# New issue order and bank assignment for a linformer attention + gated FFN kernel on Trainium2

## The chip, the cores and the metric

The kernel runs on one core of one Trainium2 chip. The metric is the device time of one execution in microseconds (us), the median of several runs. Engines are named as in the profile: PE is TensorE's matmuls and PEld its weight loads, DVE is VectorE, ACT is ScalarE, POOL is GpSimd, SP is SyncE.

## The reference

Attention with projected keys and values, and then a gated feed-forward layer on the heads joined together. Cut to what matters:

```python
# q, k, v: (8, 8, 1024, 64); E, F: (64, 1024)
k_proj = np.einsum('ks,bhsd->bhkd', E, k)
v_proj = np.einsum('ks,bhsd->bhkd', F, v)
scores = q @ k_proj.transpose(0, 1, 3, 2) / np.sqrt(64)
attn = np.exp(scores - scores.max(-1, keepdims=True))
attn = attn / (attn.sum(-1, keepdims=True) + 1e-9)
x = (attn @ v_proj).transpose(0, 2, 1, 3).reshape(8192, 512)
# w_gate, w_val: (512, 1536); w_out: (1536, 512)
gate = 1.0 / (1.0 + np.exp(-(x @ w_gate)))
out = (gate * (x @ w_val)) @ w_out          # (8192, 512), float32
```

## The kernel before

The eight batches are worked on in a software pipeline. While the feed-forward layer of one batch runs, the attention of the next is computed and the inputs of the one after that are loaded. Matmuls are in bfloat16 and add up in the eight PSUM banks `pF0..3` and `pA0..3` (128 x 512 float32 each).

Attention, per batch: GpSimd issues six loads with conversion to bfloat16 (jobs `loadkv` four times, for K and V in halves of four heads, into `KVs`; `loadq` twice, into `Qb`; L560). SyncE transposes Q by DMA (`turnq`, `qT<-Qb`). TensorE projects K and V (`kv`, `KVs,EFT`) once all four K/V halves have landed; then come the scores (`sc`), VectorE's maximum and its subtraction (`top`, `sub`), ScalarE's exponential (`exp`, into `KVs`, which then serves as `pt`), a DMA transpose (`turnp`, `eT<-KVs`), the products with V (`xo`), the division by the sum (`div`: on VectorE from PSUM, or on GpSimd from a copy in SBUF) and a second DMA transpose (`turnx`, `xT<-KVs`), which gives the layer's input `xT`. The loads of a later batch go into the same `KVs`, so they wait for the `turnx` transposes.

The feed-forward layer, per block of 512 tokens: the products with `w_gate` and `w_val` are done for six row tiles at a time with seven products of half-size blocks in place of eight (function `seven`; job names such as `GA11`, `VS3`, `GS4`). This takes sums of blocks of the input (`xs`, `xS<-xT`, four per block of tokens: one on GpSimd and three on VectorE for most blocks), additions of partial results (`plus` on VectorE, `snap` and `copy` on ScalarE), the tanh form of the sigmoid (`tanh` on ScalarE, into buffers `spare` and `EF` in SBUF) and the product gate times value (`hidden`, VectorE, L1216, `hT<-spare,...`). `hidden` reads the value from PSUM in three of the four quarters, and in the fourth (half 1, token half 1) from an SBUF buffer: then both of its inputs lie in SBUF. The output product with `w_out` is done the same way (`OA11`, `OS2` and so on), with the sums `sum1`, `sum2`, `sum3` on VectorE and `sum4` on GpSimd (L548, `hT<-hT,hS`), `merge` on VectorE and `leave` on ScalarE, and SyncE's stores of 256 KB. For the first and the last of the sixteen blocks the output product is a plain one (`Oplain`).

The order of the work is a table. The program first registers 2,902 jobs, each with its engine and its body, and then `Scheduler.run` gives every PSUM bank and SBUF buffer that a job needs its place from `PLACES` (906 entries: banks 0 to 7, buffers 0 to 12) and returns the jobs' bodies in the order of `ORDER` (2,937 entries: each job once, and 35 times -1, which stands for a filling matmul that keeps TensorE at work in the first microseconds):

```python
        for s, p in zip(slots, PLACES):
            s.at = p
        return [fill if i < 0 else self.jobs[i].body for i in ORDER]
```

`Plan.add` then derives from the order which instruction must wait for which, and each engine runs its own instructions in that order. So the table fixes five queues at once, and where a job stands among the jobs of other engines tells the time at which the table's author expects it to start.

Jobs that the prediction names, by number: loads 399, 650, 1018, 1022, 1386, 2123 (GpSimd, L560); additions 1036 and 1772 (`xs` on GpSimd, L548); `sum3` 1271, `hidden` 1565 and `sum2` 2006 (VectorE).

Of the kernel before, what the change touches and what calls it, by code (L numbers as in the profile page):

```python
# [153 lines left out]
class Job:  # L154
# [5 lines left out]
    0, -1, -1, -1, 1, 2, 3, -1, -1, -1, -1, -1, -1, 12, 4, 13, 14, 5, -1, -1, 6, 15, 16, 22, 17, -1, -1, 7, 23,  # L160
    18, 8, 19, -1, -1, -1, 24, 34, 9, 20, 25, -1, -1, 10, 32, 35, 11, 26, 33, 27, -1, -1, -1, -1, -1, -1, -1,
    -1, -1, 36, 42, 52, 37, 21, -1, -1, -1, 38, 53, 39, 43, 30, 54, 40, 28, 31, 44, 59, 55, 29, 45, 168, 41, -1,
    56, 46, 48, 57, 60, 47, 58, 169, 49, 61, -1, -1, -1, -1, 50, 62, 112, 346, 51, 119, 63, 165, 113, 64, 65,
    164, 118, 120, 174, 124, 122, 121, 126, 175, 129, 123, 128, 177, 125, 130, 178, 131, 114, 68, 116, 66, 176,
    115, 69, 67, 86, 117, 70, 87, 88, 71, 180, 76, 89, 136, 127, 96, 77, 179, 90, 144, 72, 78, 145, 181, 73, 91,
    79, 148, 146, 167, 80, 138, 133, 74, 150, 152, 92, 75, 97, 149, 93, 154, 147, 81, 140, 98, 153, 94, 166,
    142, 99, 137, 151, 95, 155, 132, 100, 82, 134, 84, 182, 101, 102, 85, 161, 103, 83, 160, 190, 184, 106, 186,
    162, 183, 104, 139, 108, 141, 107, 188, 135, 301, 105, 143, 185, 109, 302, 163, 198, 303, 111, 278, 110,
    187, 214, 199, 172, 262, 170, 304, 200, 192, 215, 171, 204, 201, 173, 216, 189, 305, 202, 217, 263, 218,
    196, 203, 220, 191, 264, 279, 395, 205, 219, 266, 265, 193, 221, 396, 206, 280, 222, 230, 207, 267, 209,  # L170
    225, 281, 210, 211, 223, 231, 269, 197, 208, 246, 212, 227, 270, 232, 226, 247, 234, 228, 233, 236, 213,
    224, 248, 235, 250, 397, 273, 251, 237, 229, 253, 308, 238, 249, 294, 254, 239, 309, 252, 398, 295, 243,
    240, 241, 255, 296, 307, 257, 244, 297, 282, 242, 256, 259, 306, 283, 537, 258, 298, 285, 260, 245, 538,
    286, 531, 299, 274, 261, 156, 300, 533, 289, 535, 158, 157, 194, 290, 323, 310, 159, 314, 319, 337, 311,
    332, 426, 315, 312, 316, 313, 320, 317, 429, 324, 318, 333, 325, 334, 326, 328, 427, 338, 423, 430, 321,
    335, 339, 322, 329, 340, 327, 539, 195, 268, 330, 424, 341, 271, 347, 331, 351, 425, 284, 431, 348, 342,
    354, 349, 275, 336, 352, 432, 355, 287, 356, 272, 357, 343, 428, 288, 350, 344, 353, 345, 276, 291, 433,
    359, 532, 366, 363, 358, 367, 360, 549, 534, 368, 361, 292, 369, 550, 277, 434, 364, 365, 362, 371, 546,
    293, 375, 378, 372, 547, 370, 373, 379, 536, 380, 540, 376, 548, 377, 381, 383, 390, 551, 374, 391, 384,
    392, 552, 385, 386, 541, 382, 553, 387, 545, 555, 393, 388, 389, 556, 543, 394, 415, 499, 557, 435, 500,  # L180
    515, 416, 436, 521, 554, 418, 501, 516, 417, 437, 439, 438, 544, 519, 517, 520, 503, 502, 505, 399, 504,
    522, 518, 440, 457, 542, 506, 523, 442, 507, 524, 526, 401, 421, 558, 419, 400, 510, 508, 528, 420, 511,
    402, 512, 529, 443, 441, 422, 509, 513, 451, 446, 527, 452, 559, 403, 444, 447, 455, 514, 525, 404, 467,
    445, 448, 530, 456, 453, 449, 483, 454, 458, 484, 473, 560, 459, 489, 487, 563, 468, 460, 561, 462, 450,
    461, 469, 488, 471, 766, 485, 463, 472, 464, 470, 474, 490, 486, 475, 669, 491, 476, 685, 670, 478, 465,
    477, 480, 492, 494, 479, 671, 493, 409, 672, 481, 686, 495, 406, 482, 466, 687, 770, 410, 496, 768, 564,
    673, 688, 405, 411, 675, 765, 674, 689, 413, 497, 691, 412, 676, 690, 498, 771, 677, 769, 407, 692, 414,
    678, 733, 693, 749, 767, 408, 734, 680, 694, 679, 682, 735, 681, 695, 696, 750, 683, 772, 736, 697, 751,
    773, 565, 737, 566, 774, 738, 752, 583, 684, 775, 567, 569, 584, 779, 776, 740, 698, 568, 570, 753, 741,
    585, 574, 578, 571, 744, 586, 780, 754, 579, 587, 572, 575, 781, 745, 573, 580, 596, 782, 756, 576, 592,  # L190
    581, 785, 562, 588, 577, 701, 757, 593, 582, 786, 702, 597, 760, 787, 589, 705, 703, 598, 590, 789, 704,
    594, 591, 739, 599, 761, 601, 790, 595, 602, 699, 603, 608, 600, 605, 706, 707, 609, 604, 606, 607, 717,
    791, 708, 700, 610, 778, 718, 617, 613, 742, 755, 709, 721, 614, 618, 611, 758, 615, 719, 722, 619, 712,
    616, 743, 612, 620, 720, 724, 625, 621, 746, 759, 622, 783, 713, 623, 747, 725, 629, 784, 626, 710, 777,
    627, 624, 728, 630, 788, 711, 714, 628, 748, 631, 637, 795, 762, 638, 796, 729, 792, 639, 715, 640, 644,
    632, 641, 793, 633, 763, 634, 716, 905, 635, 642, 645, 764, 646, 906, 647, 643, 636, 723, 794, 867, 667,
    803, 648, 868, 726, 883, 804, 869, 665, 907, 900, 730, 798, 666, 805, 870, 797, 727, 668, 871, 806, 731,
    807, 872, 819, 732, 808, 809, 899, 874, 810, 902, 875, 908, 901, 650, 811, 878, 903, 649, 873, 879, 812,
    914, 876, 651, 820, 814, 813, 816, 652, 815, 880, 817, 823, 654, 884, 881, 821, 818, 835, 653, 822, 824,
    885, 882, 887, 886, 826, 836, 904, 851, 877, 799, 837, 801, 827, 839, 888, 889, 838, 830, 909, 852, 831,  # L200
    890, 840, 911, 855, 891, 915, 913, 892, 857, 856, 800, 894, 893, 802, 858, 842, 895, 853, 843, 917, 859,
    910, 846, 916, 896, 847, 862, 912, 897, 841, 863, 918, 844, 1037, 659, 860, 845, 854, 898, 657, 861, 825,
    660, 848, 1134, 658, 864, 828, 661, 919, 849, 1038, 662, 920, 663, 829, 1039, 865, 921, 1041, 655, 850,
    1133, 832, 1040, 1053, 922, 1042, 923, 656, 833, 1054, 926, 1136, 1135, 1055, 1044, 866, 1057, 1056, 927,
    1058, 834, 924, 1137, 1043, 925, 928, 1060, 1045, 1101, 931, 1061, 1059, 1046, 930, 664, 1117, 932, 1062,
    933, 1047, 929, 1048, 934, 1064, 1049, 1138, 1050, 1102, 935, 1066, 1139, 1063, 936, 1103, 1051, 1118, 1140,
    1065, 1052, 937, 1067, 1104, 1105, 1119, 1141, 938, 1121, 1120, 946, 1122, 1142, 939, 1106, 942, 1124, 947,
    940, 1143, 943, 1125, 941, 1108, 948, 1147, 1146, 951, 1148, 1109, 944, 949, 955, 952, 1144, 1112, 945,
    1149, 953, 1113, 950, 960, 956, 1150, 964, 1069, 954, 957, 1153, 1070, 965, 1154, 958, 961, 1071, 1155, 959,
    969, 1073, 962, 1072, 1157, 970, 966, 963, 973, 1128, 971, 1068, 967, 1158, 972, 1129, 1074, 968, 976, 981,  # L210
    1085, 1159, 982, 974, 977, 1123, 975, 1086, 1076, 1126, 983, 985, 1087, 978, 986, 984, 987, 988, 1089, 989,
    993, 1088, 990, 1130, 979, 1077, 1107, 994, 1131, 995, 1145, 1000, 1080, 980, 1001, 1110, 997, 1002, 1091,
    1090, 998, 991, 1075, 999, 1092, 1078, 996, 1009, 992, 1114, 1093, 1010, 1082, 1011, 1111, 1003, 1151, 1115,
    1079, 1096, 1081, 1127, 1004, 1152, 1116, 1097, 1012, 1005, 1156, 1273, 1006, 1274, 1094, 1164, 1007, 1083,
    1160, 1008, 1275, 1013, 1098, 1132, 1014, 1235, 1015, 1033, 1171, 1236, 1161, 1016, 1172, 1034, 1237, 1084,
    1162, 1173, 1238, 1035, 1239, 1166, 1095, 1174, 1187, 1165, 1240, 1175, 1099, 1251, 1188, 1268, 1242, 1176,
    1267, 1191, 1243, 1269, 1178, 1192, 1246, 1270, 1179, 1189, 1271, 1022, 1247, 1194, 1190, 1182, 1018, 1195,
    1241, 1272, 1252, 1167, 1282, 1036, 1244, 1253, 1100, 1255, 1017, 1254, 1198, 1256, 1193, 1168, 1183, 1019,
    1177, 1258, 1180, 1020, 1248, 1259, 1196, 1276, 1245, 1021, 1249, 1184, 1257, 1025, 1199, 1262, 1185, 1203,
    1219, 1163, 1260, 1204, 1026, 1283, 1263, 1181, 1277, 1250, 1205, 1220, 1279, 1200, 1281, 1221, 1186, 1201,  # L220
# [1685 lines left out]
```

## Time and profile before

| what | value |
|---|---|
| median of three runs | 524.64 us (524.38 to 524.77) |
| the profiled execution's own time | 523.46 us |
| its span, first to last instruction | 521.7 us |
| TensorE busy in the span | 510.9 us |
| VectorE, ScalarE, GpSimd busy | 446.4, 374.5, 171.3 us |
| granted TensorE clock | 1.00 |
| DMA | 71.57 MB; 148 GB/s of HBM over the span |
| last matmul to the span's end | about 2.7 us (ScalarE's copy and the last store) |

Other lines that matter, GpSimd's groups by shape (line, engine, operation, output<-inputs, shapes, count; busy us, mean ns; idle time before them and what ended it):

```profile
L548 POOL TENSOR_TENSOR hT<-hT,hS 128x512 bf16<-128x512 bf16 x42 | 50.2, 1211 | 188.7 <-PE pF L519 87.5 <-PE pA L519 85.3 <-DVE xS L548 15.9
L548 POOL TENSOR_TENSOR xS<-xT,xS 128x512 bf16<-128x512 bf16 x14 | 16.8, 1200 | 15.0 <-DVE xS L548 15.0
L560 POOL DMA_DIRECT2D KVs<-in_k_dram x18 | 14.1, 785 | 9.4 <-DMA xT<-KVs 8.4 <-POOLq L1891 0.8 <-issue 0.2
```

How to read it: TensorE is at work nearly all the time, so the page's shares say little, and the questions are where TensorE stands still and for whom. A group's line gives the mean of all its instructions; whether a few of them are much longer is only seen in the lines of time. GpSimd's load issue is counted as busy (here 785 ns each); the transfer itself comes later and is listed from issue to landing.

### The profile page before, as it was taken

The page shows a single profiled execution, that of the slowest core. Times are in us where ns is not written, and L with a number is a line of the kernel's source. Part 1 is how long each engine was busy: PE and PEld are TensorE (multiplying, and loading weights), DVE is VectorE, ACT ScalarE, POOL GpSimd, SP SyncE. Part 2 cuts the span into 40 slices and gives each one's busy share as a digit, 9 for nine tenths or more (in the row PEclk, how much of TensorE's full clock was granted, in tenths as well). Part 3 has the DMA queues.
Part 4 walks back from the last instruction along what each step waited for, and adds up shares of the span by engine and source line. Part 5 has one row for each costly group of instructions (what it writes and reads, how often), then busy time and mean ns, then how long its engine had stood idle before and what let it go on. Part 6 is the DMA issues. An engine that isn't in the chain of part 4 may idle for free.

```text
span 521.7 us, 12142 instructions
## 1 busy us (share of the span) xinstructions
PE 510.9 (98%) x4737; PEld 426.1 (82%) x4741; DVE 446.4 (86%) x849; ACT 374.5 (72%) x714; POOL 171.3 (33%) x196
## 2 busy tenths in 40 slices
PE   8999999999999999999999799999999999999997
PEld 4556858888988998788888699888998889988875
DVE  7779997799996999979989779988899879978781
ACT  1657956788876797677966589766887678777742
POOL 9982005700553024430355013441143502503020
DMA  9999918896799644995769946698355994531104
GB/s 169 197 199 207 193 37 196 135 207 101 164 170 177 163 82 108 175 164 142 92 152 182 122 102 122 152 200 136 102 102 127 201 214 68 105 79 42 41 2 161
DMA packets 140521, 71.57 MB, mean 137 GB/s; under 512 B 97200, under 2 KB 132272, under 8 KB 140464
## 3 DMA queue, kind: packets, MB, share of 16 engines
q1 hardware_dynamic: 104560, 40.91, 38.6%
q0 software_dynamic: 35904, 29.89, 37.6%
q8 instruction: 37, 0.61, 0.5%
q14 instruction: 20, 0.16, 0.1%
HBM read 60.29 MB, written 16.78 MB: 148 GB/s over the span
## 4 chain that ended last, share of the span: by engine, by line
PE 93%; DVE 3%; ACT 1%; issue 1%; DMA 1%; DVEq 0%
PE pA L519 47%; PE pF L519 46%; DVE hT L1216 1%; DMA eT<-KVs 1%; DVE pF L1147 0%; DVE hT L1057 0%; DVE hS L548 0%; ACT spare L533 0%; ACT ost L533 0%; ACT vpD L533 0%; DVE wT L987 0%; DVE inv L980 0%; DVE ost L1405 0%; DVE EF L1147 0%; ACT EF L533 0%
## 5 line engine op out<-in xcount | busy, mean ns | idle before, releaser
L533 ACT ACTIVATE spare<-pF 128x512 f32<-128x512 f32 (+2 forms) x164 | 91.6, 570 | 30.1 <-PE pF L519 20.2
L548 POOL TENSOR_TENSOR hT<-hT,hS 128x512 bf16<-128x512 bf16 x42 | 50.2, 1211 | 188.7 <-PE pF L519 87.5
L533 ACT ACTIVATE spare<-pA 128x512 f32<-128x512 f32 (+2 forms) x150 | 86.2, 585 | 25.1 <-PE pA L519 21.6
L1725 POOL TENSOR_TENSOR KVs<-spare,inv 128x384 bf16<-128x384 f32 (+1 forms) x45 | 32.9, 739 | 91.0 <-DVE spare L1147 40.8
L1216 DVE SCALAR_TENSOR_TENSOR hT<-spare,pF 128x512 bf16<-128x512 f32 x73 | 49.5, 681 | 9.6 <-PE pA L519 3.6
L533 ACT ACTIVATE spare<-spare 128x512 f32<-128x512 f32 x73 | 45.3, 629 | 12.8 <-DVE spare L1147 12.5
L519 PE MATMUL pA<-wO,hT 128*128 128x256 bf16 (+1 forms) x358 | 51.3, 286 | 0.1
L1147 DVE TENSOR_TENSOR spare<-pA,spare 128x512 f32<-128x512 f32 x54 | 36.5, 683 | 8.8 <-ACT spare L533 5.7
L519 PEld LDWEIGHTS pA<-wO,hT 128*128 128x128 bf16 x360 | 34.9, 98 | 8.7
L1147 DVE TENSOR_TENSOR spare<-pF,spare 128x512 f32<-128x512 f32 x58 | 39.3, 683 | 3.0 <-PE pF L519 1.0
L519 PE MATMUL pF<-xT,wV 128*128 128x256 bf16 (+1 forms) x248 | 39.0, 281 | 0.0
L519 PE MATMUL pA<-xT,wG 128*128 128x256 bf16 (+1 forms) x232 | 37.5, 286 | 0.1
L519 PE MATMUL pF<-xS,tV 128*128 128x256 bf16 x248 | 36.9, 273 | 0.0
L519 PE MATMUL pF<-wO,hT 128*128 128x256 bf16 (+1 forms) x250 | 36.5, 287 | 0.1
L519 PE MATMUL pF<-xS,wV 128*128 128x256 bf16 x224 | 33.6, 273 | 2.2 <-DVE hT L1216 2.2
L1216 DVE SCALAR_TENSOR_TENSOR hT<-spare,pA 128x512 bf16<-128x512 f32 x38 | 25.9, 681 | 7.0 <-PE pA L519 4.8
L519 PE MATMUL pA<-xS,tG 128*128 128x256 bf16 x208 | 30.7, 273 | 0.0
L519 PE MATMUL pA<-xS,wG 128*128 128x256 bf16 x200 | 29.8, 272 | 0.0
L519 PEld LDWEIGHTS pF<-wO,hT 128*128 128x128 bf16 x252 | 24.5, 98 | 6.1
L519 PE MATMUL pF<-xT,wG 128*128 128x256 bf16 (+1 forms) x176 | 28.5, 285 | 0.0
L519 PE MATMUL pA<-xT,wV 128*128 128x256 bf16 (+1 forms) x160 | 27.2, 291 | 1.0 <-ACT pA L533 1.0
L519 PEld LDWEIGHTS pF<-xT,wV 128*128 128x128 bf16 x248 | 23.8, 98 | 5.4 <-issue 0.4
(183 smaller groups left out, 1294.7 us busy)
## 6 DMA issues: line engine op xcount, KB each, us to landing
out_dram<-ost SPq DMA_DIRECT2D x63, 256.0 KB, 2.5
KVs<-in_v_dram POOLq DMA_DIRECT2D x15, 512.0 KB, 11.9
KVs<-in_k_dram POOLq DMA_DIRECT2D x14, 512.0 KB, 9.0
Qb<-in_q_dram POOLq DMA_DIRECT2D x14, 512.0 KB, 12.9
wO<-in_moe_w_out_dram POOLq DMA_DIRECT2D x1, 1536.0 KB, 28.9
wG<-in_moe_w_gate_dram POOLq DMA_DIRECT2D x5, 256.0 KB, 16.4
wV<-in_moe_w_val_dram POOLq DMA_DIRECT2D x5, 256.0 KB, 17.0
KVs<-in_k_dram POOLq DMA_DIRECT2D x4, 256.0 KB, 6.2
```

The lines of the kernel that those rows point to most:

```text
L519: lambda e: e.matmul(o, lhsT, rhs, **kw),
L533: lambda e: e.activation(o, i, func, scale=scale),
L548: fn = lambda e: e.tensor_tensor(o, a, b, op)
L1147: lambda e: e.tensor_tensor(PB(b)[:, :] if stay else BF(s), PB(b)[:, :], BF(s), ALU.add),
L1216: lambda e: e.scalar_tensor_tensor(o, y.rearrange("p (j c) -> p j c", j=2), 1.0, x.rearrange("p (j c) -> p j c", j=2), ALU.add, ALU.mult,),
L1725: fn = lambda e: e.tensor_tensor(xto.rearrange("p (g h d) -> p h g d", g=2, h=H)[:, hh[0] : hh[1], :, :], o[:, :, 0:DH].rearrange("p (h g) ...
```

## The change

Only the two tables are new. `ORDER` differs at 2,619 of its 2,937 places and `PLACES` at 811 of 906; both keep their lengths, the new `ORDER` holds the same jobs once each, and there are 35 filling matmuls again, some of them at other places among the first hundred entries. Every other line of the program is the same. The tables come from a search whose model of time counts how GpSimd's additions, alone or queued behind the issue of a load, hold up VectorE.

The diff, cut to rows of `ORDER` that hold the jobs named above (each row is 18 to 29 jobs in order):

```diff
 ORDER = (
...
-    807, 872, 819, 732, 808, 809, 899, 874, 810, 902, 875, 908, 901, 650, 811, 878, 903, 649, 873, 879, 812,
...
-    1267, 1191, 1243, 1269, 1178, 1192, 1246, 1270, 1179, 1189, 1271, 1022, 1247, 1194, 1190, 1182, 1018, 1195,
-    1241, 1272, 1252, 1167, 1282, 1036, 1244, 1253, 1100, 1255, 1017, 1254, 1198, 1256, 1193, 1168, 1183, 1019,
...
-    1552, 1567, 1588, 1655, 1634, 1538, 1568, 1589, 1553, 1591, 1386, 1565, 1554, 1653, 1392, 1569, 1592, 1648,
...
-    1978, 2011, 1989, 2006, 1992, 1755, 1913, 1979, 1990, 1994, 1758, 1820, 1835, 2018, 1995, 1772, 1916, 1982,
...
+    824, 909, 886, 836, 822, 890, 912, 826, 801, 891, 851, 839, 650, 889, 840, 910, 894, 892, 882, 837, 895,
...
+    1267, 1188, 1242, 1176, 1269, 1189, 1243, 1178, 1022, 1099, 1191, 1179, 1282, 1036, 1100, 1192, 1182, 1190,
+    1252, 1246, 1019, 1271, 1183, 1194, 1247, 1167, 1020, 1241, 1195, 1255, 1244, 1018, 1193, 1256, 1169, 1198,
...
+    1616, 1386, 1556, 1552, 1617, 1613, 1630, 1390, 1468, 1559, 1618, 1625, 1640, 1560, 1557, 1535, 1628, 1577,
...
+    1648, 1569, 1653, 1595, 1537, 1573, 1575, 1574, 1654, 1576, 1590, 1593, 1578, 1596, 1773, 1579, 1570, 1659,
...
+    1778, 1870, 1392, 1586, 1658, 1874, 1599, 1393, 1780, 1396, 1565, 1789, 1602, 1662, 1397, 1869, 1837, 1790,
...
+    1769, 1907, 1771, 1752, 1971, 1851, 1908, 2010, 1770, 1852, 1831, 1909, 1900, 1772, 1911, 1899, 1867, 1910,
+    1897, 1912, 1868, 1987, 1972, 1914, 2004, 1988, 1898, 1973, 1915, 1975, 2003, 1902, 1974, 1991, 1901, 2006,
...
+    1982, 1995, 1836, 1920, 1983, 1755, 2007, 1918, 1923, 1921, 1919, 1758, 1998, 1924, 1977, 1999, 2019, 2008,
...
 )
```

In these rows 1386, 1022, 1018, 1755, 1758 and 650 are load issues of GpSimd; 1648, 1036 and 1772 are its additions; 1271, 1565 and 2006 are VectorE's; 1282, 1653 and 1654 are products of TensorE.

347 rows, old and new, of tables (ORDER, PLACES) are left out of this document.

## The prediction, made before the run

> **What bounds the kernel now.** I read the page's engine totals first, then the waits of TensorE, then the lines of time around the longest ones, and last VectorE's and GpSimd's groups.
>
> The first line of part 1:
>
> ```profile
> PE 510.9 (98%) x4737; PEld 426.1 (82%) x4741; DVE 446.4 (86%) x849; ACT 374.5 (72%) x714; POOL 171.3 (33%) x196
> ```
>
> TensorE is busy for 98% of the span and the chain of waits is 93% TensorE, so time can come only out of its gaps. The waits of TensorE (engine and tile, whom it waited for, total us, times, longest):
>
> ```profile
> PE pF L519 <- DVE hT L1216: 2.9, 2, 2.2
> PE pF L519 <- issue: 1.2, 2, 0.8
> ...
> PE pA L519 <- ACT pA L533: 1.0, 1, 1.0
> PE pA L519 <- DVE hS L548: 0.4, 1, 0.4
> ```
>
> The reader is to see that a handful of single waits make up nearly all of it. A matmul of 256 columns starts 0.109 us after the one before it when nothing holds TensorE, so a gap is the distance of two starts less 0.109 us for each matmul between. Lines of time of TensorE in three windows (start, duration):
>
> ```profile
> 212.47 0.82 PE L519 MATMUL pA<-wT,hS 128*128 128x256 bf16 x6
> 214.30 0.61 PE L519 MATMUL pA<-xT,wV 128*128 128x256 bf16 x4 [1.01 <-ACT pA L533]
> ...
> 295.54 0.82 PE L519 MATMUL pF<-wO,hT 128*128 128x256 bf16 x6
> 297.13 2.01 PE L519 MATMUL pF<-KVs,EFT 128*64 128x512 bf16 x16 [0.78 <-issue]
> ...
> 338.09 0.60 PE L519 MATMUL pA<-wT,hS 128*128 128x256 bf16 x4
> 339.08 0.39 PE L519 MATMUL pA<-wT,hS 128*128 128x256 bf16 x2 [0.39 <-DVE hS L548]
> ```
>
> 214.30 - 212.47 - 6 x 0.109 is 1.18 us lost; 297.13 - 295.54 - 0.65 is 0.94; 339.08 - 338.09 - 0.44 is 0.55. By the same rule 0.85 us are lost before the start at 341.47, and the largest gap is in this window, all engines:
>
> ```profile
> 284.76 0.79 POOL L560 DMA_DIRECT2D KVs<-in_k_dram  x1
> ...
> 284.98 3.41 DVE L1216 SCALAR_TENSOR_TENSOR hT<-spare 128x512 bf16<-128x512 f32 x1
> ...
> 285.56 2.27 POOL L548 TENSOR_TENSOR hT<-hT,hS 128x512 bf16<-128x512 bf16 x2
> ...
> 287.02 0.60 PE L519 MATMUL pA<-xS,tV 128*128 128x256 bf16 x4
> ...
> 289.85 0.61 PE L519 MATMUL pF<-xS,wV 128*128 128x256 bf16 x4 [2.23 <-DVE hT L1216]
> ```
>
> 289.85 - 287.02 - 0.44 is 2.39 us. VectorE's instruction, which began while GpSimd issued a load, ended 0.56 us after the second of the two additions queued behind that load. The five gaps sum to 1.18 + 2.39 + 0.94 + 0.55 + 0.85 = 5.91 us. Which instructions are so held, the groups of VectorE show (busy us, mean ns | idle before, released by):
>
> ```profile
> L1216 DVE SCALAR_TENSOR_TENSOR hT<-spare,pF 128x512 bf16<-128x512 f32 x73 | 49.5, 681 | 9.6 <-PE pA L519 3.6 <-ACT spare L533 2.9 <-PE pF L519 2.0
> L1216 DVE SCALAR_TENSOR_TENSOR hT<-spare 128x512 bf16<-128x512 f32 x32 | 26.4, 826 | 0.2
> ```
>
> One reading PSUM (`pF`) keeps 681 ns; one with both inputs in SBUF (`spare` alone, job `hidden` of half 1, token 1) averages 826. Held alike are the jobs `sum1` to `sum3` and VectorE's `xs`. After 60 us I count 13 held instructions, 10.5 us over their usual durations. Three stand behind a load with an addition after it (jobs 1271 at 210.80: 2.23 for 0.69; 1565 at 284.98: 3.41 for 0.69; 2006 at 336.89: 2.13 for 0.69), and after exactly these TensorE has the gaps at 213, 287, 338 and 340. The ten held by an addition or product of GpSimd alone lose 0.07 to 0.9 us each, 4.8 in all, and no gap above 0.25 us follows any of them.
>
> The fifth gap, at 296, is another matter: the K/V projection waits for that same load, job 1386, which took 12.3 us to land:
>
> ```profile
> DMA to landing us min/median/max: 12.3/12.3/12.3
> ```
>
> **The change, part by part.** Both lists hold the same 2,902 jobs once each and 35 filling matmuls, and no job changes its engine: TensorE's 4,741 weight loads and their matmuls stay, as do 56 later additions and 68 load issues of GpSimd. Cost of that: nothing. Banks and buffers: `spare<-pA,spare` and `spare<-pF,spare` both take 683 ns, so a place costs nothing by itself.
>
> To compare the lists I put each job at the TensorE work listed ahead of it (0.109 us per 256-column matmul, 0.216 per 512, 0.056 per 128) plus 11.0 us; I call it list time. From 30 us to 213 the old list's time is within 0.9 us of the trace.
>
> *The three places behind a load.* At list time 282.6 the old list has load 1386, `hidden` 1565 next to it, and two additions. The new one puts 1386 at 274.6 between other loads, and 1565 at 293.7, with no GpSimd addition within 9 us. At 330.9 load, load, addition 1772 beside `sum2` 2006 becomes 1772 at 326.3 and then six loads in a row. At 210.8 `sum3` 1271 beside load 1022, load 1018, addition 1036 becomes 1022, 1036 with VectorE on PSUM work, and 1271 after them. Pairs of a load and an addition straight behind it are not fewer (I count 8 against 6), but in the listed order no two-input VectorE job stands beside the issue in any of the 8, except where the addition waits for that very job (224.3, 406.7). If the order is kept in time: -1.18, -2.39, -0.55, -0.85, together -4.97 us.
>
> *The late load.* All four K/V loads of that batch now stand 17 to 20.5 us ahead of their projection, against 12.3 us to land: -0.94 us.
>
> *What comes back.* GpSimd does not keep list time: with TensorE's lag taken off, its groups of loads began ahead of their list time in the trace, at 150.3 by 1.7 us, at 210.8 by 1.3, at 271.5 by 1.7, at 330.9 by 1.1, and at 393.8 by 0. Advanced by 1.3 us, load 1022 (list time 209.9) and addition 1036 (211.0) start at about 208.6 and 209.7, where the new list has two `sum2`, and the product OS2 at 210.4 reads their result. That is the arrangement of the 1.18 us gap of before: I charge 1.2. At 271 to 272.6 the second load and an addition, 1.7 us ahead, would touch another `sum2`; the overlap is about even, so 0.6. Bounds: 0 and 2.4 us for the two. Behind a held instruction VectorE's whole queue stands, and with it ScalarE's copies and TensorE's next product. Small waits elsewhere: 0.1. Together +1.9.
>
> *SP's queue and the start.* Transposes keep their leads: shortest from `turnp` to its reader 3.5 us in both lists (landing 3.1, median), from `turnq` to the scores 4.6 before, 5.0 now (landing 4.6). The two eT gaps of before (0.2 and 0.4 us) bound this at -0.6 to +0.8; I take 0. In the first 48 us one K half is moved behind a Q load (GpSimd's queue); loads landed in issue order until 61.4 us, so it should land at about 58.5, 1.6 us before its projection. TensorE's gaps of over 0.1 us from waits there sum to about 2.3, so -2.3 to +2.3; I take 0, as nothing in the list favours a side.
>
> Sum: span 521.7 - 4.97 - 0.94 + 1.9 = 517.7 us. The profiled execution took 523.46 with 1.76 us around its span, so 519.5; the median of the runs is 1.18 above that execution, which makes **520.6**.
>
> A rule that speaks against this: the Trainium skill, "SBUF — State Buffer", section "Who interferes with whom", says that a VectorE instruction with two SBUF inputs and a GpSimd instruction reading SBUF exclude each other, that the one issued first keeps the ports for its whole length, and infers that descriptor generation does not take the port such a VectorE instruction needs. By it the instruction at 284.98, begun 0.58 us before the additions, should have ended in 0.69. The trace has 3.41, so the measurement decides. Were the rule right, there would be nothing to gain behind loads, which is the second rival.
>
> **The rivals.** (1) GpSimd runs ahead so often that the holds behind loads return as before: only the late load's 0.94 is gained, 523.7. For it: 8 such pairs and the advance of 1.1 to 1.7 us at most load groups. Against: at 97.6, 157.7 and 282.2 VectorE has PSUM jobs all around, and the additions after 224.3 and 406.7 wait for a VectorE `xs` anyway. (2) The holds do not depend on what stands behind a load but fall by chance, as often with the same additions and the same two-input jobs: the 5.91 us recur elsewhere, 524.6. Against: three of three long holds have that form.
>
> (3) Slower: other loads become the late ones. The new list leaves 8.1 us from load 650 (157.7) to its projection, 10.0 from 2123 (403.4) and 10.9 from 399 (100.7); the old one had 12.0 or more except for 1386 with 8.5. If each takes the 12.3 us of 1386, TensorE waits 4.2 + 2.3 + 1.4 = 7.9 us: 528.5. It decides from a landing of 11.0 us at all three (2.9 + 1.0 + 0.1 eats the 4.0 gained). For: loads queued behind others landed after 7.6 to 18.6 us. Against: 1386 was in flight with two `qT` transposes issued 0.09 and 1.37 us after it, while 650 and 399 come ahead of their Q loads; the first load of a group lands in 5.6 to 7.4.
>
> **How the numbers follow.** Chances: forecast 0.61, rival 1 0.16, rival 2 0.07, rival 3 0.16. The likeliest one's own range is 518.7 (all 5.91 gone, nothing back) to 522.9 (2.4 at the two places, the start 1.0 and transposes 0.8 to the bad). For 8 in 10 I reach a little below, to 518.0, for a luckier start, and up to 525.0, which takes in rivals 1 and 2 and the mild part of rival 3. A measurement of this kernel tells about 0.2%, 1.05 us, from no change. Faster by more: the forecast and most of rival 1 less a little, 0.76; within: rival 2 and edges, 0.08; slower: 0.16.
>
> **What would show it.** Right: VectorE's `hT<-spare` group near 700 to 750 ns, no instruction of it over 2 us, TensorE's waits for `hT L1216` below 1 us, and no gap before the projection near 290. The step that brings 1.2 back is right if VectorE's `sum2` near 208 to 210 us lasts over 1.5 us with a gap of about 1 us after it. Wrong: holds of 2 us at other loads (rival 1), or waits of over 1 us before `pF<-KVs,EFT` or `pA<-KVs,EFT` (rival 3). Prediction: 520.6 us, range 518.0 to 525.0; faster 0.76, same 0.08, slower 0.16.

## The result, and the profile after

| | before | after |
|---|---|---|
| median of the runs | 524.51 us (524.25 to 524.77, 4 runs) | 518.85 us (518.57 to 519.34, 4 runs) |
| profiled execution | 523.46 us | 518.57 us |
| its span | 521.7 us | 516.8 us |

The ratio is 0.9893, 95% interval 0.9876 to 0.991. The new lists make the kernel 5.7 us faster.

The page's engine totals after:

```profile
PE 510.5 (99%) x4741; PEld 426.6 (83%) x4741; DVE 436.6 (84%) x849; ACT 374.4 (72%) x714; POOL 169.8 (33%) x196
```

TensorE has the same work as before. VectorE, with the same 849 instructions, is busy 9.8 us less. About 7.5 us of that is time in which its instructions with two inputs in SBUF stood still (11.6 us over the usual durations of their shapes before, 4.1 after, over the whole span). The waits of TensorE after (engine, tile and line, whom it waited for; total us, times, longest):

```profile
PE pA L518 <- DMA KVs<-in_k_dram: 1.1, 2, 0.9
PE pA L518 <- DVE tV L642: 1.1, 1, 1.1
PE pA L518 <- DVE xT L876: 0.5, 1, 0.5
```

The list is cut to its three longest. The 2.9 us for VectorE's `hT`, the 1.0 for ScalarE's `pA` and the 0.4 for `hS` are gone from it (line numbers are one lower than before). The second line is the fixed start, which stood there before as well. The first line is new. It lies in this window of TensorE:

```profile
229.73 0.60 PE L518 MATMUL pF<-xT,wV 128*128 128x256 bf16 x4
231.22 1.99 PE L518 MATMUL pA<-KVs,EFT 128*64 128x512 bf16 x16 [0.88 <-DMA KVs<-in_k_dram]
```

231.22 - 229.73 - 4 x 0.109 is 1.05 us lost: the projection of one batch waits for its last K/V half. It is the one gap above 0.2 us that TensorE has after the first 50 us. VectorE's group that the prediction pointed to (busy us, mean ns | idle before):

```profile
L1215 DVE SCALAR_TENSOR_TENSOR hT<-spare,pF 128x512 bf16<-128x512 f32 x60 | 40.8, 679 | 7.7 <-PE pF L518 3.7 <-ACT spare L532 3.5
L1215 DVE SCALAR_TENSOR_TENSOR hT<-spare 128x512 bf16<-128x512 f32 x33 | 24.1, 731 | 0.8 <-ACT spare L532 0.7
```

Reading PSUM it takes 679 ns as before; with both inputs in SBUF the mean falls from 826 to 731. After 60 us, 13 instructions were held before, 11.4 us over the usual (median) durations of their shapes; now there are 7, with 3.7 us in all and the longest lasting 1.63 us. None of them begins during a load issue with an addition straight behind it.

Where the 4.86 us between the two spans went, by distances of starts: the five gaps of the prediction, -5.91; the new one near 230, +1.05; the first 50 us, about +0.7 (of it 0.42 at 48 us, where TensorE waits for a copy into `xT`); the eT gaps near 257 and 262 and one near 123, -0.73. The sum is about -4.9. The medians differ by 5.66 because the profiled execution of before was 1.05 us below its runs' median and the one after 0.28 below.

### The profile page after: what moved, and what is told of

Read it like the earlier page. It is cut to its first block, busy times and chain, and to the rows that moved or that the text cites. A ratio compares the mean times of both kernels' runs of the same rounds, so it can differ in the third digit from the quotient of the medians.

```text
span 516.8 us, 12171 instructions
## 1 busy us (share of the span) xinstructions
PE 510.5 (99%) x4741; PEld 426.6 (83%) x4741; DVE 436.6 (84%) x849; ACT 374.4 (72%) x714; POOL 169.8 (33%) x196
## 4 chain that ended last, share of the span: by engine, by line
PE 55%; DMA 3%; issue 1%; POOL 1%; ACT 0%; POOLq 0%
PE pF L518 28%; PE pA L518 27%; DMA KVs<-in_k_dram 3%; POOL KVs L559 0%; POOL Qb L559 0%; ACT ost L532 0%; POOL xS L547 0%; POOLq L129 0%
## 5 line engine op out<-in xcount | busy, mean ns | idle before, releaser
L532 ACT ACTIVATE spare<-pF 128x512 f32<-128x512 f32 (+2 forms) x167 | 94.2, 574 | 32.0 <-PE pF L518 22.7
L1724 POOL TENSOR_TENSOR KVs<-spare,inv 128x384 bf16<-128x384 f32 (+1 forms) x41 | 29.6, 731 | 84.4 <-DVE topf L1635 35.3
L1146 DVE TENSOR_TENSOR spare<-pF,spare 128x512 f32<-128x512 f32 x59 | 40.1, 681 | 10.5 <-PE pF L518 5.2
L1215 DVE SCALAR_TENSOR_TENSOR hT<-spare,pF 128x512 bf16<-128x512 f32 x60 | 40.8, 679 | 7.7 <-PE pF L518 3.7
L518 PE MATMUL pA<-wO,hT 128*128 128x256 bf16 (+1 forms) x336 | 47.2, 280 | 0.0
L1215 DVE SCALAR_TENSOR_TENSOR hT<-spare,pA 128x512 bf16<-128x512 f32 x52 | 35.3, 678 | 8.3 <-PE pF L518 4.1
L518 PE MATMUL pF<-wO,hT 128*128 128x256 bf16 (+1 forms) x276 | 42.2, 296 | 0.0
L518 PE MATMUL pA<-xS,wV 128*128 128x256 bf16 x248 | 37.2, 273 | 0.0
L518 PE MATMUL pF<-xS,wG 128*128 128x256 bf16 x232 | 34.1, 272 | 0.0
L518 PE MATMUL pF<-xS,tV 128*128 128x256 bf16 x224 | 33.6, 273 | 0.0
L532 ACT ACTIVATE EF<-pA 128x512 f32<-128x512 f32 (+2 forms) x35 | 19.7, 564 | 14.4 <-PE pA L518 13.5
```

Source lines behind the costliest of these rows:

```text
L518: lambda e: e.matmul(o, lhsT, rhs, **kw),
L532: lambda e: e.activation(o, i, func, scale=scale),
L1146: lambda e: e.tensor_tensor(PB(b)[:, :] if stay else BF(s), PB(b)[:, :], BF(s), ALU.add),
L1215: lambda e: e.scalar_tensor_tensor(o, y.rearrange("p (j c) -> p j c", j=2), 1.0, x.rearrange("p (j c) -> p j c", j=2), ALU.add, ALU.mult,),
L1724: fn = lambda e: e.tensor_tensor(xto.rearrange("p (g h d) -> p h g d", g=2, h=H)[:, hh[0] : hh[1], :, :], o[:, :, 0:DH].rearrange("p (h g) ...
```

## The experiments

What had to be told apart: do the three long holds come from what stands beside VectorE in GpSimd's queue (a load issue with an addition behind it), and is that the gain; or do holds fall by chance, with the gain coming from the 2,600 other places and the new banks? All edits of the lists use one helper put behind the table:

```diff
+def moved(order, *moves):
+    order = list(order)
+    for job, behind in moves:
+        order.remove(job)
+        order.insert(order.index(behind) + 1, job)
+    return tuple(order)
```

e1 to e4 share a chip and its runs of the kernel before, with a median of 524.43 us; e5 to e7 and the new kernel again share another, with 523.80. Each ratio is to the kernel before on the same chip.

**e1: the old list, load 1386 moved ahead.**

```diff
+ORDER = moved(ORDER, (1386, 1388))
```

> The old list with one job moved: load 1386 behind load 1388, so that `hidden` 1565 no longer starts during a load issue with two additions behind it, and the load comes about 8 us earlier. Theory (a two-input VectorE instruction that begins during a load issue is held through all additions queued behind that load): 1565 is held by one addition at most, 1.2 to 1.8 us in place of 3.41, the gap of 2.39 us near 287 falls to 0 to 0.6 and the 0.94 before the projection at 296 is gone: 2.7 to 3.3 us faster, 521.2 to 521.8. Rival (holds fall by chance, wherever the load stands): 1565 stays above 2.5 us and only the 0.94 is gained, 523.6.

Measured: 520.34 us, ratio 0.9926 (0.9903 to 0.9949), so 4.1 us faster, with 2.7 to 5.1 in the interval. That is more than the 2.7 to 3.3 us that were expected. GpSimd, TensorE and VectorE around `hidden` 1565, start and duration:

```profile
285.01 2.71 POOL L558 TENSOR_TENSOR hT<-hT,hS 128x512 bf16<-128x512 bf16 x2
...
285.24 1.48 DVE L1226 SCALAR_TENSOR_TENSOR hT<-spare 128x512 bf16<-128x512 f32 x1
...
287.28 0.60 PE L529 MATMUL pA<-xS,tV 128*128 128x256 bf16 x4
...
288.18 0.50 PE L529 MATMUL pF<-xS,wV 128*128 128x256 bf16 x3 [0.30 <-DVE hT L1226]
```

The same VectorE instruction meets the same two additions, back to back. With the load issue ahead of them it took 3.41 us, to 0.56 after the second; without it 1.48 us, and it gets in after the first. (It began 0.23 us after the first addition here, and 0.58 us before it in the kernel before.) TensorE's gap falls from 2.39 to 0.46 us (288.18 - 287.28 - 0.44) and the one before the projection is gone: 2.87 us together, inside the interval. The traced execution is the slowest of the six, 522.11 us: near 429 us TensorE lost 1.24 us there waiting for a DMA into `kpD`; the other traces show 0.2 at most there. The rival, which left 1565 above 2.5 us, falls.

**e2: the old list, two additions ahead of their loads.**

```diff
+ORDER = moved(ORDER, (1036, 1034), (1772, 1770))
```

> The old list with two jobs moved: additions 1036 and 1772 ahead of their groups of loads instead of between the loads. Theory: `sum3` 1271 and `sum2` 2006, which then begin beside loads with only loads behind them, keep 0.69 us, and the gaps of 1.18 (213), 0.55 and 0.85 (338, 340) go: 2.6 us faster, 521.9, with up to 0.5 us given back where the moved additions hold another VectorE job alone. Rival (by chance): the gaps recur nearby, within 0.5 us of 524.5.

Measured: 521.58 us, ratio 0.9948 (0.9928 to 0.9968), 2.85 us faster, as expected. Here the loads stay beside VectorE and the addition behind them is gone. First the kernel before, VectorE and then GpSimd:

```profile
210.80 2.23 DVE L548 TENSOR_TENSOR hT<-hT 128x1024 bf16<-128x1024 bf16 x1
...
210.54 0.75 POOL L560 DMA_DIRECT2D KVs<-in_k_dram  x1
211.29 1.18 POOL L548 TENSOR_TENSOR xS<-xT,xS 128x512 bf16<-128x512 bf16 x1
```

Then e2, GpSimd and VectorE:

```profile
210.12 0.81 POOL L570 DMA_DIRECT2D Qb<-in_q_dram  x1 [2.44 <-DMA xT<-KVs]
210.92 1.50 POOL L570 DMA_DIRECT2D KVs<-in_k_dram  x2
```

```profile
211.08 0.68 DVE L558 TENSOR_TENSOR hT<-hT 128x1024 bf16<-128x1024 bf16 x1
```

`sum3` 1271 begins 0.16 us into a load issue (0.26 before), and takes 0.68 us in place of 2.23. So the issue alone holds nothing. The ten traces of this case bear that out: after 60 us, 95 VectorE instructions with two inputs in SBUF began during a load issue with another load straight behind it, and none was held. The gaps at 213, 338 and 340 are gone, and the 2.38 us ahead of 288.87 stand as they were, since 1386 is untouched. A small one is new, 0.39 us ahead of 356.38, where the projection waits for a K/V half.

**e3: the old list, all three moved.**

```diff
+ORDER = moved(ORDER, (1386, 1388), (1036, 1034), (1772, 1770))
```

> The old list with all three jobs moved (1386, 1036, 1772), 2,899 left as they were. Theory: 4.97 + 0.94 us less 0 to 0.6 returned at 287, so 518.6 to 519.5, the new kernel's time. Rival (the new list gains by its many other moves and by its banks): at most half of the gain, 521.7 or more.

Measured: 518.22 us, ratio 0.9887 (0.9866 to 0.9909), 6.2 us faster, at least what the new list gains (0.9893, 0.9876 to 0.991) and 0.4 us better than the expected range. Three jobs of 2,902 moved, with the old banks, give the whole gain: the other moves and the banks aren't needed for it. VectorE's `hT<-spare` group falls from a mean of 826 ns to 767 by 1565 alone, which takes 1.48 us in place of 3.41: one addition still holds it. Its gap of 0.47 us is the largest after 50 us; the next, 0.36 at 353, is a wait for a K/V half.

**e4: the new list, one addition moved back behind a load.**

```diff
+ORDER = moved(ORDER, (1772, 1757))
```

> The new list with one job moved back: addition 1772 right behind load 1757, beside `sum2` 2006. Theory: the `sum2` that begins near 331.9, 0.4 us after the load issue's start, is held until the addition ends, 1.7 to 2.0 us in place of 0.42, VectorE's queue is 1.4 us late and TensorE's product of hS near 334.0 starts 0.3 to 1.2 us late: 519.1 to 520.0. Rival (who starts first keeps the ports): `sum2` keeps 0.42 to 0.7 us, the addition takes longer instead, and the time stays at 518.85.

Measured: 519.49 us, ratio 0.9904 (0.9884 to 0.9925). The new kernel's lines first, then those of e4:

```profile
331.50 0.81 POOL L559 DMA_DIRECT2D Qb<-in_q_dram  x1 [1.43 <-DMA xT<-KVs]
...
331.91 1.02 DVE L547 TENSOR_TENSOR hS<-hS,hT 128x512 bf16<-128x512 bf16 x2
...
332.30 0.75 POOL L559 DMA_DIRECT2D KVs<-in_v_dram  x1
```

```profile
332.61 0.80 POOL L569 DMA_DIRECT2D Qb<-in_q_dram  x1 [5.45 <-issue]
...
332.73 2.43 DVE L557 TENSOR_TENSOR hS<-hS,hT 128x512 bf16<-128x512 bf16 x2
...
333.43 1.17 POOL L557 TENSOR_TENSOR xS<-xT,xS 128x512 bf16<-128x512 bf16 x1
...
334.38 0.60 PE L528 MATMUL pA<-xS,tV 128*128 128x256 bf16 x4
...
335.21 0.33 PEld L528 LDWEIGHTS pF<-wT,hS 128*128 128x128 bf16 x4 [0.51 <-DVE hS L557]
335.21 0.50 PE L528 MATMUL pF<-wT,hS 128*128 128x256 bf16 x3 [0.23 <-DVE hS L557]
```

Two `sum2` instructions, 2006 and then 2005, take 1.02 us together beside two loads, and 2.43 us when an addition stands behind the first load. The hold can be brought back: 2005 began at 333.07, during the issue and 0.36 us before the addition, and lasted 2.09 us, to 0.56 us after the addition's end. Who starts first doesn't decide here. TensorE starts 0.39 us late (335.21 - 334.38 - 0.44). The theory said 1.7 to 2.0 us and 0.3 to 1.2.

But the theory named the other job. 2006 began at 332.73, 0.12 us into the same issue, and was not held: it kept its 0.42 us. In the kernel before, the same job began 0.09 us into an issue with an addition straight behind it and took 2.13. So an issue with an addition behind it holds most instructions that begin beside it, seven of the eight in the ten traces, but not all, and what spared this one is not shown.

The time alone would not settle it: it is 0.64 us above the new kernel's first median, and the ranges of the runs overlap.

**e5 to e7 and the new kernel again: the one new gap.** The gap near 230 hangs on four K/V loads which come behind a Q load and an addition.

```diff
+ORDER = moved(ORDER, (1036, 1034))                  # e5
+ORDER = moved(ORDER, (1022, 1017))                  # e6
+ORDER = moved(ORDER, (1036, 1034), (1022, 1017))    # e7
```

> The new list with addition 1036 moved ahead of load 1022, so that the four K/V loads of that batch are issued 1.2 us sooner. The new kernel's one large gap (1.05 us near 230, TensorE's projection waiting for the last K/V half, landed at 231.17). Theory A (the half is late because its issue is late): it lands about 1.2 us sooner, the gap is below 0.2 us, 517.8. Theory B (it is late because the transfers stand in line behind the Q load and beside the Q transposes): it lands within 0.4 us of before and the gap stays, 518.9.

> The new list with load 1022 (Q) moved behind the four K/V loads of its group, so that no Q load stands ahead of them and its transposes start later. Theory B: the last K/V half lands 3 us sooner or more, before 228, the gap near 230 is gone: 517.8 or less. Theory A: the issue of the halves is 0.8 us sooner at most, so the gap shrinks to 0.2 to 0.5 and the time to 518.2. If the later Q transposes are late for their scores, a new gap of up to 1 us stands near 234 to 245.

> The new list with both moves. By either theory the gap near 230 is gone; 517.6 to 517.9, unless the Q transposes come late (then a gap near 234 to 245).

> The new kernel once more, beside the three others on the same chip: 518.85 give or take 0.5, with the gap near 230 between 0.5 and 2 us from one execution to another, since it hangs on transfers.

| run | median us (range) | last K/V half issued, landed | gap near 230 |
|---|---|---|---|
| after_again | 518.13 (517.62 to 520.19) | 214.25, 230.76 | 1.10 |
| e5 | 517.69 (516.98 to 518.31) | 212.82, 228.56 | none |
| e6 | 517.27 (517.15 to 517.78) | 213.34, 225.42 | none |
| e7 | 517.20 (516.84 to 517.46) | 212.31, 224.80 | none |

TensorE in e7 at that place:

```profile
229.49 0.60 PE L528 MATMUL pF<-xT,wV 128*128 128x256 bf16 x4
230.01 1.92 PE L528 MATMUL pA<-KVs,EFT 128*64 128x512 bf16 x16
```

Both theories have a part. With the addition out of the way (e5) the last half is issued 1.43 us sooner and lands 2.2 sooner; with the Q load behind it as well (e7) it lands another 3.8 us sooner. e6 alone doesn't separate them: addition 1036, no longer behind the load that waits for the `turnx` transposes, ran early there too. No gap at the scores came from the later Q transposes. e7 has the lowest median: ratio to the kernel before 0.9873 (0.9843 to 0.9903), and 0.93 us below the new kernel on the same chip, all of its four runs below all six of that one. e6, 0.07 us above it, can't be told apart from it. The new kernel itself came out at 518.13, 0.7 us below its first median and outside the 0.5 that were allowed; the kernel before was as much faster on this chip (523.80 against 524.51). The size of the gap in the new kernel varies with the transfers: 1.05, 1.10 and, in e4's execution, 1.99 us.

## Why the prediction was right

**What bounds the kernel** held: the changes of TensorE's gaps add up to the change of the span, about -4.9 us.

**The three places behind a load, -4.97 us.** Right in size, and in cause: e1 and e2 take away the load or the addition, and the long hold goes with either; e4 puts an addition back, and a hold returns. One detail was too good in e1 and e3 alone: there 1565 still meets an addition, and 0.46 us of its gap stay. In the new list 1565 stands far from any addition, and nothing stays. Two readings were off without touching the forecast: the shape of 2006 usually takes 0.42 us, not 0.69, and by the usual durations of their shapes the 13 held instructions lost 11.4 us, not 10.5 (the ten held by GpSimd's additions and products alone 5.4, up to 0.97 each).

**The late load, -0.94 us.** Right: the last K/V half of that batch landed at 285.90 and its projection began at 293.86.

**What comes back, +1.9 us.** This is the term that was mis-sized, and nothing of it came where it was put. I charged 1.2 us because GpSimd would run 1.3 us ahead of its list at load 1022 and put addition 1036 beside two `sum2`, at 208.6 and 209.7. They started at 210.43 and 211.26, by the same reckoning only about 0.15 us ahead: the `turnx` transpose that the load waits for landed 4.28 us after its issue, where that of before took 3.04. The two `sum2` took 0.68 and 0.69 us, and the 0.6 near 271 did not come either. What did come back is 1.05 us at 230, of the kind of rival 3 (a K/V load too late), but at a load that the rival doesn't name: load 1017 was issued at 214.61, about 15.6 us before the projection could have begun, and landed 16.6 us after its issue. I had looked at the shortest distances only, though the 7.6 to 18.6 us that I gave for queued loads covers this one. It stands at the edge of the sign that was written down for rival 3, waits of over 1 us before a projection: 0.88 in the list of waits, 1.05 by the starts.

**SP's queue and the start, 0.** The eT gaps of before (0.57 us) were not met in the new kernel's profile, and the first 50 us cost about 0.7 more; both lie within the bounds that were given.

**The sum.** 3.9 us were forecast for the span, 4.86 came; 520.6 for the median, 518.85 came. About 1 us of that difference is the term above and the rest is the step from one profiled execution to the median: 1.18 us were added, of which the new kernel showed 0.28. That another gap of 1.05 us came in place of the 1.8 that were charged at the two places is luck for the sum.

**The rivals.** Rival 1 (the holds return at other loads) and rival 2 (they fall by chance, 5.91 us as before) are refuted by the profile after and by e1 to e4. The rule that was weighed there, of the Trainium skill's "SBUF — State Buffer", section "Who interferes with whom", is borne out where no load issue is under way: 95 times in the ten traces GpSimd began an addition or product while such a VectorE instruction ran, and the VectorE instruction kept its usual time, while an addition took up to 1.71 us in place of 1.16. The load issue alone holds nothing either (e2). That the one which starts first goes first fails beside a load issue with an addition straight behind it: 3.41, 2.23, 2.13 and, in e4, 2.09 us. Rival 3 didn't occur at its three loads: load 650 landed 8.2 us after its issue, 2123 8.2 and 399 9.6, below the 11.0 from which it would have decided.

## What to carry to other kernels

When a kernel is bound by one engine at 98%, list that engine's few gaps by the distances of its starts and look at each with all engines side by side; three jobs moved were worth as much as a whole new order. A group's mean hides holds: the mean of 826 ns in one of `hidden`'s groups of before came from a few held ones, the longest 3,409 ns; compare the maximum, and compare instructions that read PSUM with those that have both inputs in SBUF. Before crediting a large reordering with its gain, move the two or three suspected jobs alone.

## What the runs showed of the hardware

In these traces every hold of more than 1 us beyond the usual time had both a load issue under way when the VectorE instruction began and an addition straight behind that issue: with a load behind it `sum3` took 0.68 us, with one addition 2.23, and `hidden` with two additions 3.41, to 0.56 us after the last of them ended. With an addition behind the issue seven of eight were held, with a load behind it none of 95, and with an addition that began without a load issue none of 95; many of these are the same jobs in different runs. Between two additions with no load issue ahead, VectorE got in after the first (1.48 us). Why an addition that has not begun can hold an instruction that has, and why 2006 was spared in e4, these runs don't show; that the addition has not begun rests on GpSimd's recorded starts, and the profile calls its spans on GpSimd rough.

Within a group of loads, a load's time to land grew with the loads that were issued just ahead of it. The five loads of the group at 210 us of the new kernel, Q first and then four K/V halves, landed 6.3, 8.5, 11.7, 14.0 and 16.6 us after their issue; in e7, with Q last, the four halves took 5.8, 7.6, 9.4 and 12.5 us. Why the fourth load of e7 is faster than the fourth of the new kernel, these runs don't separate.
